# Where the scratch writes of weights stand in a fused attention and gated-MLP kernel

## The chip, the cores and the metric

The kernel runs on one core of a Trainium2 chip. Its time is the device time of one execution in microseconds (us), a median over runs. The core has TensorE (matrix products; in the profile PE, with its weight loads as PEld), VectorE (DVE), ScalarE (ACT), GpSimd (POOL, almost unused here) and SyncE (SP), whose queue issues nearly all DMAs. SBUF is the memory on the core, PSUM holds the sums that TensorE writes, and DRAM scratch tiles are memory outside the core that the kernel writes and reads again.

## The reference

Chunked attention with a left and right context and eight memory keys, and then RMS normalisation and a gated MLP over its output. All is in 32 bit floats.

```python
for c in range(nc):                       # 24 chunks of 32 queries, for 4 batches x 8 heads
    ...
    scores = scale * np.matmul(q_c, k_full.transpose(0, 1, 3, 2))     # 8 memory keys + up to 56
    scores = scores - np.max(scores, axis=-1, keepdims=True)
    a = np.exp(scores)
    a = a / (np.sum(a, axis=-1, keepdims=True) + 1e-09)
    out[:, :, c_start:c_end] = np.matmul(a, v_full)
...
x = out.transpose(0, 2, 1, 3).reshape(3072, 512)
rms = np.sqrt(np.mean(x * x, axis=-1, keepdims=True) + 1e-06)
xn = x / rms * rms_g
g = xn @ w_gate                           # 512 x 1536
silu = g * (1.0 / (1.0 + np.exp(-g)))
val = xn @ w_val                          # 512 x 1536
return (silu * val @ w_out).astype(np.float32)        # 1536 x 512
```

## The kernel before

**Tiling.** The 3072 tokens are eight blocks of 384. The 1536 hidden features are twelve groups of 128, `f` = 0 to 11. Each fp32 factor is split in a high and a low part, and a product is three passes (high-high, high-low, low-high). For a block, each `f` needs a gate product (tile `pg`, L469), a value product (`pv`, L469), an activation (tanh L483, then VectorE's L487, L490 and the split into `hh` and `hl`, L178 and L499), and an output product (`po`, L519).

**Four parts in order of time.** (1) Blocks 0 and 1, with their attention, by a list of steps written out by hand (`ORDER`); also the weights are split here. (2) The loop over `segments`: the rest of block 0 (f 5 to 11, seven features), all of block 2 (the third block), all of block 3. (3) Blocks 4 and 5 together (`whole(2)`), with a Strassen-like scheme of sums, and then (4) blocks 6 and 7 (`whole(3)`). Parts 3 and 4 read their weights back from DRAM scratch tiles `kept` through a ring of 30 buffers `r`. The scratch tiles are filled during part 2.

**What fills the scratch tiles.** There are twelve items, one for each pair of features `p` (0 to 5) and each of the gate and value weights (`g`, `v`). An item has a plain part and a split part:

- `dumps(k)` writes the plain part: six DMAs straight from the split weights in SBUF (four of `kg` or `kv`, 256 and 128 KB, and two of `ko`, 256 KB; 1280 KB in all; L767). They wait for nothing but their place in SyncE's queue: each call is tied behind the last SyncE instruction written so far. Their order is items 2 to 11, then 0 and 1 (the pair of features 10 and 11).
- `keep_steps` makes the split part, in eight steps an item: two additions (VectorE, L803), four quarter steps (VectorE, L806; after the fourth ScalarE copies into `kh`, L810), and two subtractions (L815), the last of them with two DMAs of 512 KB (L817 from `kh`, L819 from `ks` or `qp`). `kh` is a single buffer. The sums alternate between two buffers (`ks` and a part of `qp`). The last two steps of an item come after the first two of the next. A step has a size (512, or 256 for a quarter step), and `keep(n)` draws steps until `n` is used up.

**Gaps and visits.** In part 2, `visit(2 * n)` comes after the gate product of the n-th feature of the block, `visit(2 * n + 1)` after its value product, and `visit(2 * n + 1.5)` after the output product of the feature before. These places are called gaps. At a gap stand, in this order, `dumps`, `keep` and steps of the attention of later blocks, by `VISITS`: "p" (transposes `pT`, L279), "s" (the scores of a pair of units, L216, then loads of queries and keys of the next pair into the same buffers, L163 and L165), "o" (the outputs `oe` and `oo`, L310, and loads of values, L170) and "n" (steps of the normalisation). The query and key buffers (`q`, `qp`, `kv`) exist once for each unit of a pair, so a load waits until the scores of the pair before have been read.

**What sets the order.** TensorE's instructions keep the program's order. For VectorE, ScalarE and SyncE a planner orders them at build time by a simulated timeline, within the dependencies, the priorities and the ties that the program gives (`tc.issue_after`). On the chip each engine runs its own list in order.

`KEEP[blk][gap]` holds the sizes for `keep`. The plain parts have no table; `visit` says

```python
if blk == 0 and gap in range(12):
    dumps((gap + 2) % 12)
keep(KEEP[blk].get(gap, 0))
```

Of the kernel before, what the change touches and what calls it, by code (L numbers as in the profile page):

```python
# [8 lines left out]
F32 = mybir.dt.float32  # L9
# [14 lines left out]
DM, FF = 512, 1536  # L24
P = 128
# [22 lines left out]
NR = 30  # L48

KEEP = {0: {2: 1024, 3: 1024},  # L50
# [3 lines left out]

CHAIN = (("g", 1, "a", 1), ("g", 2, "c", 1), ("v", 1, "a", 1), ("g", 6, "a", 0), ("v", 2, "c", 1), ("g", 7, "a", 0),
         ("v", 6, "a", 0), ("g", 5, "e", 1), ("g", 4, "a", 0), ("v", 7, "a", 0), ("g", 3, "e", 0), ("v", 5, "e", 1),
# [30 lines left out]
def tile_kernel(ctx: ExitStack, tc: tile.TileContext, q, k, v, w_gate, w_val, w_out, rms_g, out):  # L87
# [11 lines left out]
    dram = ctx.enter_context(tc.tile_pool(name="dram", bufs=1, space=bass.MemoryType.DRAM))  # L99
# [174 lines left out]
    def stage_p(u, tag=None):  # L274
        d = st[u]
        t = psum_m(tag, f"pT{u}") if tag else psum_a(f"pT{u}")
        pe = d["p"].rearrange("p j k -> p (j k)")
        for i in range(NT):
            on_pe(nc.tensor.transpose(out=t[:, i * P:(i + 1) * P], in_=pe[:, i * P:(i + 1) * P], identity=ident))  # L279
        d["t"] = t  # L280
# [183 lines left out]
    def moe_in(n, f, xs, kts=range(NKT), ps=None):  # L464
        if ps is None:
            ps = psum_m(n, f"p{n}")
        for kt in kts:
            for i, (a, c) in enumerate(PASS):
                on_pe(nc.tensor.matmul(ps[:, 0:HT], lhsT=weight(a, n, f, kt), rhs=xs[c][:, kt],  # L469
                                 start=kt == 0 and i == 0, stop=kt == NKT - 1 and i == 2))  # L470
        return ps[:, 0:HT]
# [37 lines left out]
    def moe_h(g, vv, blk):  # L509
        t = moe_t(g, vv, blk)  # L510
        return moe_hl(t, moe_hh(t))

    def psm_o(i):
        return psum_m(f"o{i}", f"po{i}")

    def moe_out(f, h, po, first=0, end=NF - 1):
        for i in range(NT):
            for n, (a, c) in enumerate(PASS):
                on_pe(nc.tensor.matmul(po[i], lhsT=h[a][:, i * P:(i + 1) * P], rhs=weight(c, "o", f),  # L519
                                 start=f == first and n == 0, stop=f == end and n == 2))  # L520
# [4 lines left out]
    def store(blk, po):  # L525
        for i in range(NT):
            o = obuf(f"ob{i}")
            nc.scalar.activation(o, po[i], AF.Copy, scale=0.5 if blk > 1 else sh[blk][:, i:i + 1])
            nc.scalar.dma_start(out=out[blk * HT + i * P:blk * HT + (i + 1) * P], in_=o)
# [23 lines left out]
    def last_of(eng):  # L553
        return next(i for i in reversed(nc.cur_bb.bb.instructions) if i.engine == eng.engine)
# [136 lines left out]
    def tok_o(n):  # L691
# [10 lines left out]
        P=lambda n: stage_p(n, "o0" if n < NG else None),  # L702
# [58 lines left out]
    kept = {}  # L761

    def dump(f, w, cols, to):
        k, i, n = fgroup[f]
        for part in range(2):
            c = wt[part, w, k].bitcast(F32)[:, i * DM:(i + 1) * DM]
            nc.sync.dma_start(out=to[:, :, part], in_=c[:, cols].rearrange("p (k f) -> p k f", k=to.shape[1]))  # L767

    items, sums = [(p, w) for p in (5, 0, 1, 2, 3, 4) for w in "gv"], {}

    def dumps(k):
        p, w = items[k]
        fa, fb = PAIRS[p]
        kept[w, p] = t = dram.tile([P, 7, 2, DM // 2], F32, name=f"k{w}{p}")
        with tc.issue_after(last_of(nc.sync)):
            dump(fa, w, slice(0, DM), t[:, 0:2])
            dump(fb, w, slice(DM // 2, DM), t[:, 2:3])
            f = fa if w == "g" else fb
            kept["o", f] = t = dram.tile([P, 2, DM], F32, name=f"ko{f}")
            dump(f, "o", slice(0, DM), t.unsqueeze(1))  # L780

    def keep_steps():

        late_part = iter(())
        for k in range(len(items) + 1):
            now = keep_item(k) if k < len(items) else iter(())
            for _ in range(2):
                if k < len(items):
                    yield next(now)
            yield from late_part  # L790
            if k < len(items):
                for _ in range(4):
                    yield next(now)
            late_part = now

    def keep_item(k):
        p, w = items[k]
        fa, fb = PAIRS[p]
        s = (late["tmp"] if k % 2 else p1.tile([P, 2 * DM], F32, name="ks", tag="wy")).rearrange("p (k f) -> p k f", k=4)
        for i, f in enumerate((fb, fa)):  # L800
            c, n, _ = fgroup[f]
            h, l = (wt[part, w, c][:, n * DM:(n + 1) * DM].bitcast(F32).rearrange("p (k f) -> p k f", k=2) for part in range(2))
            nc.vector.tensor_tensor(out=s[:, 2 * i:2 * i + 2], in0=h, in1=l, op=ALU.add)  # L803
            yield DM
        for o, a, b, op in ((1, 0, 1, ALU.add), (0, 2, 0, ALU.subtract), (2, 1, 2, ALU.subtract), (3, 3, 2, ALU.subtract)):
            nc.vector.tensor_tensor(out=s[:, o], in0=s[:, a], in1=s[:, b], op=op)  # L806
            if o == 3:
                h = p1.tile([P, 3 * HT], F32R, name="kh", tag="rg")[:, 0:2 * DM].rearrange("p (k f) -> p k f", k=4)
                for i in range(4):
                    nc.scalar.copy(h[:, i], s[:, i])  # L810
            yield DM // 2
        l, t = s.bitcast(F32R), kept[w, p]
        for i in range(2):
            c = slice(2 * i, 2 * i + 2)
            nc.vector.tensor_tensor(out=l[:, c], in0=s[:, c], in1=h[:, c].bitcast(F32), op=ALU.subtract)  # L815
            if i:
                nc.sync.dma_start(out=t[:, 3:7, 0], in_=h.bitcast(F32))  # L817
                with tc.issue_after(last_of(nc.sync)):
                    nc.sync.dma_start(out=t[:, 3:7, 1], in_=s)  # L819
            yield DM  # L820

    keeping = keep_steps()

    def keep(n):
        with tc.issue_after(last_of(nc.vector)), tc.issue_after(last_of(nc.scalar)):
            while n > 0:
                n -= next(keeping, DM)
# [150 lines left out]
    for blk, fs in segments:  # L978
        po = [psm_o(i) for i in range(NT)] if blk else sp["po", 0]
        edge = dict(first=fs[0] if blk else 0, end=fs[-1])  # L980

        def visit(gap):
            if blk == 0 and gap in range(12):
                dumps((gap + 2) % 12)
            keep(KEEP[blk].get(gap, 0))
            for c in VISITS[blk].get(gap, ""):
                if next(todo) != c:
                    raise AssertionError(gap)
        for n, f in enumerate(fs):
            g = moe_in("g", f, xs)  # L990
            visit(2 * n)
            out_ = lambda f=fs[n - 1], h=prev: moe_out(f, h, po, **edge)
            if n == 0:
                out_ = lambda: None
                if blk == 0:

                    moe_out(NF - 1, prev, po1)
                    with tc.high_priority():
                        store(1, po1)
            vv = moe_in("v", f, xs)  # L1000
            visit(2 * n + 1)
            if n < len(fs) - 1:
                out_()
                visit(2 * n + 1.5)
                prev = moe_h(g, vv, blk)
                if blk == 3 and n == 2:
                    late_cm[1].__exit__(None, None, None)
                if blk == 3 and n == 7:
                    w0_cm.__exit__(None, None, None)
                    xpool = ctx.enter_context(tc.tile_pool(name="xs", bufs=1, reuse_waits="tile"))  # L1010
                    sup["ring"] = ctx.enter_context(tc.tile_pool(name="ring", bufs=NR, reuse_waits="tile"))
                    for m in (1, 2, 3, 6):
                        sup["xpool", m] = xpool
                    load(NR)
                    x_first(4)
                if blk == 3 and n == 9:
                    x_second(4)
            elif blk < 3:
                with tc.high_priority():
                    t = moe_t(g, vv, blk)  # L1020
                xs = split_x(late_x["x"], t, out_, lambda h: moe_out(fs[-1], h, po, **edge))
            else:
                with tc.high_priority():
                    h = moe_h(g, vv, blk)
                out_()
        if blk == 0:
            behind.close()
        if blk < 3:
            store(blk, po)
# [84 lines left out]
```

## Time and profile before

| | |
|---|---|
| median of 3 runs | 696.56 us (696.29 to 696.63) |
| the profiled execution | 696.32 us, of which the span from first to last instruction is 694.5 us |
| granted TensorE clock, mean | 0.993 |
| TensorE busy | 667.8 us (96%) |
| VectorE, ScalarE busy | 471.5 us (68%), 305.0 us (44%) |
| DMA queue of SyncE | 77760 packets, 136.08 MB, 58.6% of 16 engines' span |
| the stage from 147.2 to 212.75 us (rest of block 0) | 65.55 us; TensorE busy 59.76, VectorE 41.43, ScalarE 20.22; DMA engines 98% busy, 335 GB/s |

The page gives busy times by engine, then 40 equal slices of the span, each with its busy share in tenths (here 17.4 us a slice), then DMA queues, the chain of work that ended last, and the costliest groups of instructions. Lists of waits say who waited for whom: total us, how often, and the longest. A timeline's row has start, duration, engine (SPq is SyncE's DMA queue, where the duration is that of issuing), line of the kernel, operation and tiles (written <- read), count, and in brackets the idle time before it with what ended it. A table of stretches has the length, then busy time of TensorE, its weight loads, VectorE, ScalarE and GpSimd with counts, then the granted TensorE clock, the DMA share and GB/s.

### The profile page before, as it was taken

What the parts mean: (1) busy time and instruction counts of PE and PEld (TensorE: products, weight loads), DVE (VectorE), ACT (ScalarE), POOL (GpSimd) and SP (SyncE); (2) the same over time, 40 slices, a digit from 0 to 9 for tenths busy, and PEclk for the clock granted to TensorE, in tenths of its full rate; (3) what the DMA queues carried; (4) which work ended last, traced back from release to release, by engine and by line L of the source; (5) the groups of instructions that cost most, each with busy time, mean ns of one, the idle gap of its engine ahead of it and who ended that gap; (6) DMA issues with size and microseconds to landing.
All of it is one profiled execution on the core that took longest, in us unless ns stands there. A gap on an engine that the chain in (4) does not pass through costs nothing.

```text
span 694.5 us, 15083 instructions
## 1 busy us (share of the span) xinstructions
PE 667.8 (96%) x6134; PEld 609.5 (88%) x6134; DVE 471.5 (68%) x937; ACT 305.0 (44%) x566; POOL 4.7 (1%) x12
## 2 busy tenths in 40 slices
PE   7799999999699999999999999999999999999997
PEld 6698899998598898889999899998988899999885
DVE  6788999867478898867858766569639254555221
ACT  4787987832235444344234444343334343332112
POOL 0010000000000000000000000000000000000000
PEclk9999999999999999999999999999999999999999
DMA  9653643449996746337139688887643598885002
GB/s 326 248 179 126 238 156 106 148 153 371 322 375 233 232 152 203 116 99 254 58 108 356 234 255 282 266 294 237 192 143 123 177 301 252 251 254 160 0 1 91
DMA packets 79701, 140.19 MB, mean 202 GB/s; under 512 B 7440, under 2 KB 33040, under 8 KB 79632
## 3 DMA queue, kind: packets, MB, share of 16 engines
q1 hardware_dynamic: 77760, 136.08, 58.6%
q10 hardware_dynamic: 1872, 3.15, 1.2%
q8 instruction: 48, 0.79, 0.5%
q14 instruction: 21, 0.17, 0.1%
HBM read 104.60 MB, written 34.60 MB: 200 GB/s over the span
## 4 chain that ended last, share of the span: by engine, by line
PE 75%; DVE 11%; DMA 5%; ACT 5%; issue 2%; SPq 1%; ACTq 0%; DVEq 0%
PE po L957 14%; PE pv L469 10%; PE pg L469 10%; PE po L519 10%; PE mga L928 7%; PE mva L928 7%; PE mve L928 3%; PE mge L928 3%; PE oe L310 2%; PE mvc L928 2%; PE s L216 2%; PE pT L279 2%; DMA r<-kg 1%; PE mgc L928 1%; DVE t L487 1%
## 5 line engine op out<-in xcount | busy, mean ns | idle before, releaser
L957 PE MATMUL po<-r,hhs 128*128 128x512 f32 x288 | 90.7, 396 | 0.0
L469 PE MATMUL pv<-xh,wh_v 128*128 128x384 f32 x192 | 65.8, 343 | 2.2 <-DVE t L490 1.3
L469 PE MATMUL pg<-xh,wh_g 128*128 128x384 f32 x192 | 66.7, 347 | 0.4 <-DVE t L487 0.4
L469 PE MATMUL pg<-xl,wh_g 128*128 128x384 f32 x192 | 65.4, 341 | 0.5 <-DVE xl L654 0.5
L469 PE MATMUL pv<-xh,wl_v 128*128 128x384 f32 x192 | 65.1, 339 | 0.5 <-DVE wl_v L440 0.5
L469 PE MATMUL pg<-xh,wl_g 128*128 128x384 f32 x192 | 65.5, 341 | 0.0
L469 PE MATMUL pv<-xl,wh_v 128*128 128x384 f32 x192 | 65.1, 339 | 0.0
L957 PEld LDWEIGHTS po<-r,hhs 128*128 128x128 f32 x288 | 53.9, 188 | 12.4
L519 PE MATMUL po<-wh_o,hh 128*128 128x512 f32 x144 | 58.3, 405 | 0.8 <-ACT hh L753 0.4
L928 PE MATMUL mga<-x,r 128*128 128x384 f32 x288 | 58.3, 337 | 0.2 <-ACT spare L900 0.2
L928 PE MATMUL mva<-x,r 128*128 128x384 f32 x288 | 58.1, 337 | 0.1
L519 PE MATMUL po<-wh_o,hl 128*128 128x512 f32 x144 | 57.4, 398 | 0.0
L519 PE MATMUL po<-wl_o,hh 128*128 128x512 f32 x144 | 57.2, 397 | 0.0
L957 PE MATMUL po<-r,hls 128*128 128x512 f32 x144 | 56.8, 395 | 0.0
L939 DVE TENSOR_TENSOR hls<-h,hhs 128x768 fp32r<-128x768 f32 x24 | 22.9, 955 | 42.1 <-ACT hhs L938 42.1
L928 PEld LDWEIGHTS mga<-x,r 128*128 128x128 f32 x288 | 50.5, 188 | 1.0 <-ACT spare L900 0.5
L928 PEld LDWEIGHTS mva<-x,r 128*128 128x128 f32 x288 | 50.5, 188 | 0.5 <-DVE h L911 0.4
L178 ACT CAST hh<-t 128x384 fp32r<-128x384 f32 x46 | 23.7, 514 | 47.4 <-PE po L519 35.7
L938 ACT CAST hhs<-h 128x768 fp32r<-128x768 f32 x24 | 20.0, 835 | 54.4 <-PE po L957 50.5
L469 PEld LDWEIGHTS pv<-xh,wh_v 128*128 128x128 f32 x192 | 36.3, 189 | 4.0 <-DVE t L490 1.6
L469 PEld LDWEIGHTS pg<-xh,wh_g 128*128 128x128 f32 x192 | 36.3, 189 | 2.8 <-DVE t L487 0.9
L469 PEld LDWEIGHTS pg<-xl,wh_g 128*128 128x128 f32 x192 | 36.4, 189 | 2.1 <-DVE xl L654 0.7
(162 smaller groups left out, 1424.6 us busy)
## 6 DMA issues: line engine op xcount, KB each, us to landing
r<-kg SPq DMA_DIRECT2D x84, 256.0 KB, 3.3
r<-kv SPq DMA_DIRECT2D x84, 256.0 KB, 3.3
r<-ko SPq DMA_DIRECT2D x48, 256.0 KB, 3.1
kv<-in_v_dram SPq DMA_DIRECT2D x24, 384.0 KB, 5.3
kv<-in_k_dram SPq DMA_DIRECT2D x24, 312.0 KB, 4.7
ws<-in_moe_w_gate_dram SPq DMA_DIRECT2D x4, 1024.0 KB, 4.9
ws<-in_moe_w_val_dram SPq DMA_DIRECT2D x4, 1024.0 KB, 4.9
ws<-in_moe_w_out_dram SPq DMA_DIRECT2D x4, 1024.0 KB, 5.0
```

Of the source, the lines that this page charges most:

```text
L178: return nc.scalar.copy(out, in_)
L216: on_pe(nc.tensor.matmul(d["s"][a:a + CH, o:o + KC], lhsT=d["q"][r, c * CH:c * CH + CH], rhs=d["k"][r, c // 2, 40 * cp:40 * cp + KC], star ...
L279: on_pe(nc.tensor.transpose(out=t[:, i * P:(i + 1) * P], in_=pe[:, i * P:(i + 1) * P], identity=ident))
L310: on_pe(nc.tensor.matmul(o2[cp][64 * hh:64 * hh + 64, o:o + CH], lhsT=st[u]["v"][r, j, hh], rhs=pt[r, j, hh ^ u % 2], start=True, stop=True))
L469: on_pe(nc.tensor.matmul(ps[:, 0:HT], lhsT=weight(a, n, f, kt), rhs=xs[c][:, kt], start=kt == 0 and i == 0, stop=kt == NKT - 1 and i == 2))
L487: nc.vector.scalar_tensor_tensor(out=t, in0=t, scalar=1.0, in1=g, op0=ALU.add, op1=ALU.mult)
L519: on_pe(nc.tensor.matmul(po[i], lhsT=h[a][:, i * P:(i + 1) * P], rhs=weight(c, "o", f), start=f == first and n == 0, stop=f == end and n = ...
L928: on_pe(nc.tensor.matmul(bank[w, b], lhsT=r[:, a, kt], rhs=x[:, c, kt], start=bool(first) and kt == 0 and i == 0, stop=kt == 1 and i == 2, ...
L938: nc.scalar.copy(hh, sup["h", f])
L939: nc.vector.tensor_tensor(out=hl, in0=sup["h", f], in1=hh.bitcast(F32), op=ALU.subtract)
L957: on_pe(nc.tensor.matmul(po[i], lhsT=cur[a][:, i * P:(i + 1) * P], rhs=r[c], start=f == n == 0, stop=f == NF - 1 and n == 2))
```

## The change

The items still go out in the same order, but by a table `DUMPS` of gaps. Before, gaps 0 to 11 of block 0 each had an item. Now gaps 0, 1, 2 and 6 to 12 of block 0 have the first ten, and gaps 1 and 2 of block 2 have the two of features 10 and 11. The scratch tiles are named ahead of the loop. The table `KEEP` has other sizes in blocks 2 and 3, so that some steps of the split parts move by a gap or more; their sequence is the same. Which steps a gap draws, from the generator, where they differ most (the item's pair and weight, then the step):

| gap | before | after |
|---|---|---|
| block 2, gap 0 | 5v first addition | 5v both additions |
| block 2, gap 16 | 3v four quarter steps, 4g additions | 3g last subtraction and write, 3v two quarter steps |
| block 2, gap 18 | 3v first subtraction | nothing |
| block 3, gap 2 | 3v last subtraction and write, 4g two quarter steps | 3v two quarter steps, 4g additions |
| block 3, gap 3 | 4g two quarter steps, 4v additions, 4g first subtraction | 3v subtractions and write, 4g four quarter steps |
| block 3, gap 4 | 4g last subtraction and write, 4v four quarter steps and first subtraction | 4v additions |
| block 3, gap 6 | 4v last subtraction and write | 4g first subtraction |
| block 3, gap 10 | nothing | 4g last subtraction and write, 4v four quarter steps, subtractions and write |

```diff
 KEEP = {0: {2: 1024, 3: 1024},
-        2: {0: 512, 1: 2048, 2: 2048, 3: 2048, 4: 2048, 6: 512, 7: 1024,
-            8: 2048, 9: 2048, 10: 2048, 11: 2048, 12: 2048, 13: 2048, 14: 2048, 15: 2048, 16: 2048, 18: 512},
-        3: {2: 1024, 3: 2048, 4: 2048, 6: 512, 10: 1024}}
+        2: {0: 1024, 1: 2048, 2: 2048, 3: 2048, 4: 1024, 6: 512, 7: 1024, 8: 2048, 9: 2048, 10: 2048, 11: 2048, 12: 2048, 13: 2048,
+            14: 2048, 15: 2048, 16: 1024},
+        3: {2: 1536, 3: 2048, 4: 1024, 6: 512, 10: 3072}}
+
+DUMPS = {0: (0, 1, 2, 6, 7, 8, 9, 10, 11, 12), 2: (1, 2), 3: ()}
...
-    items, sums = [(p, w) for p in (5, 0, 1, 2, 3, 4) for w in "gv"], {}
+    items = [(p, w) for p in (5, 0, 1, 2, 3, 4) for w in "gv"]
+    for p, w in items:
+        kept[w, p] = dram.tile([P, 7, 2, DM // 2], F32, name=f"k{w}{p}")
 
     def dumps(k):
+        k = (k + 2) % len(items)
         p, w = items[k]
         fa, fb = PAIRS[p]
-        kept[w, p] = t = dram.tile([P, 7, 2, DM // 2], F32, name=f"k{w}{p}")
+        t = kept[w, p]
         with tc.issue_after(last_of(nc.sync)):
...
-    keeping = keep_steps()
+    keeping, dumping = keep_steps(), iter(range(len(items)))
...
         def visit(gap):
-            if blk == 0 and gap in range(12):
-                dumps((gap + 2) % 12)
+            if gap in DUMPS[blk]:
+                dumps(next(dumping))
             keep(KEEP[blk].get(gap, 0))
```

## The prediction

> **What bounds the kernel now.** I read the page first, then TensorE's list of waits, then the stretch around its longest wait in the timelines of TensorE and SyncE. The page:
>
> ```profile
> span 694.5 us, 15083 instructions
> PE 667.8 (96%) x6134; PEld 609.5 (88%) x6134; DVE 471.5 (68%) x937; ACT 305.0 (44%) x566; POOL 4.7 (1%) x12
> PE   7799999999699999999999999999999999999997
> DVE  6788999867478898867858766569639254555221
> DMA  9653643449996746337139688887643598885002
> ```
>
> TensorE is busy 96% of the span, so only its idle time is to be won. Between its first and its last slices it falls in one alone, the eleventh (174 to 191 us), to 6; there VectorE falls to 4 and the DMA engines stand at 9. That is the stage in which block 0's last part runs and all the scratch writes are issued. Its waits, over the whole run (total, times, longest):
>
> ```profile
> PE s L216 <- DMA kv<-in_k_dram: 5.3, 2, 3.8
> ...
> PE pv L469 <- ACT xT L321: 0.8, 1, 0.8
> ```
>
> The first row is two waits, 5.3 us in sum, of an attention pair's scores for a key load. TensorE's timeline and the chain that ended last show two visits that do the same work, gap 5 (no wait) and gap 7 (both waits):
>
> ```profile
> 169.95 0.82 PE L279 MATMUL pT<-ident,pe 128*128 128x128 f32 x6
> ...
> 180.24 0.82 PE L279 MATMUL pT<-ident,pe 128*128 128x128 f32 x6
> 184.86 0.30 PE L216 MATMUL s<-kv,q 64*32 64x64 f32 x4 [3.79 <-DMA kv<-in_k_dram]
> 186.68 0.32 PE L216 MATMUL s<-kv,qp 64*32 64x64 f32 x2 [1.52 <-DMA kv<-in_k_dram]
> ...
> 192.79 0.44 PE L469 MATMUL pg<-xh,wh_g 128*128 128x384 f32 x1
> ```
> ```profile
> 170.76 1.10 PE s L216 x72
> 171.87 2.31 PE po L519 x9
> ...
> 175.97 2.31 PE pg L469 x12
> ...
> 180.65 5.89 DMA kv<-in_k_dram
> ...
> 186.68 1.58 PE s L216 x87
> 188.25 2.99 PE po L519 x9
> ```
>
> From the transposes to the next gate matmul, gap 5 takes 175.97 - 169.95 = 6.02 us and gap 7 192.79 - 180.24 = 12.55 us. The difference, **6.53 us**, is what the waits cost: 3.79 + 1.52 = 5.31 us of waiting and 1.22 us of slower work behind it. SyncE's queue says why the load was late:
>
> ```profile
> 162.94 0.38 SPq L767 DMA_DIRECT2D kg<-wh_g  x1
> ...
> 166.71 0.50 SPq L767 DMA_DIRECT2D kv<-wh_v  x1
> ...
> 179.19 0.40 SPq L163 DMA_DIRECT2D q<-in_q_dram  x1
> ...
> 181.18 0.85 SPq L170 DMA_DIRECT2D kv<-in_v_dram  x2
> 182.08 0.73 SPq L767 DMA_DIRECT2D kg<-wh_g  x1
> ...
> 191.78 0.41 SPq L163 DMA_DIRECT2D q<-in_q_dram  x1
> ...
> 194.78 1.04 SPq L767 DMA_DIRECT2D kg<-wh_g  x1
> ...
> 212.31 0.37 SPq L817 DMA_DIRECT2D kg<-kh  x1
> ```
>
> The pair's buffers come free at 171.87, when gap 5's scores end. The loads leave only from 179.19 on, since SyncE works in order and until then issues the items of gaps 3, 4 and 5 (from 166.71). The last key load leaves at 180.65 and takes 5.89 us; the scores could have begun at 184.86 - 3.79 = 181.07.
>
> **The change part by part.** Times go against the profiled execution: 694.5 us of span, 696.32 us in all. The median of the runs, 696.56, is 0.24 above it.
>
> *Removed* from in front of the loads: the items of gaps 3, 4 and 5, 18 DMAs. Gap 2's item is out by 166.7; SyncE then waits for the scores, and the last key load leaves 180.65 - 179.19 = 1.5 us after the first, at 173.4. How long loads and writes of this buffer took in this stage, at least, in the middle and at most:
>
> ```profile
> DMA to landing us min/median/max: 2.9/4.6/6.8
> ```
>
> At the worst the last key lands at 180.2, before 181.07: both waits go. The value loads behind wait for the end of gap 5's output matmuls (175.97), are issued by 176.9 and land by 183.7 at the worst; gap 7's output needs them 1.10 + 2.31 us after 181.1, at 184.5. So nothing is late next in this visit. The slower work goes with the wait, as the granted clock (third from the end) says:
>
> ```profile
> 186.70:188.30 1.60, 1.60 (x93) 1.43 (x93) 0.04 (x1) 0.00 (x0) 0.00 (x0) 0.50 1.06 383
> 188.30:191.20 2.90, 2.90 (x13) 2.06 (x13) 1.91 (x4) 0.68 (x2) 0.00 (x0) 0.75 1.08 389
> ```
>
> After the idle time the clock is 0.50, then 0.75; the scores took 1.58 for 1.10 us and the output 2.99 for 2.31. The Trainium skill (TensorE: Matmul & The Clock Gate, Part 1: The HAM clock gate) says that one idle window of about 3.4 us halves the clock and that about 3.4 us of sustained work restores it. By its figure the slow stretch would cost 3.4 x 0.5 = 1.7 us, an estimate, and the visit 7.0 us in place of 6.53; the rows are shorter, and they decide. Term: **-6.53**. VectorE lets TensorE keep it: at 4 tenths in this slice it has no backlog, and the norm chain behind gap 7 begins with TensorE's outputs, so it moves along.
>
> *Moved:* five items (six DMAs each) now follow gap 7's loads, in gaps 8 to 12, and one each stands in block 2's gaps 1 and 2. Only the last stage reads them. But the first write of split parts (kh, the row at 212.31) is queued behind gap 1's item, the second behind gap 2's too, and kh has one buffer: ScalarE's next copies into it wait until the write has landed. ScalarE, VectorE, TensorE and the landing times of kh's writes:
>
> ```profile
> 220.48 0.71 ACT L810 CAST kh<-qp 128x256 fp32r<-128x256 f32 x2
> 221.58 0.49 ACT L483 ACTIVATE t<-pg 128x384 f32<-128x384 f32 x1 [0.39 <-PE pg L469]
> ```
> ```profile
> 223.56 0.55 DVE L487 SCALAR_TENSOR_TENSOR t<-t,pg 128x384 f32<-128x384 f32 x1
> ...
> 277.88 1.29 DVE L803 TENSOR_TENSOR ks<-wh_g,wl_g 128x512 f32<-128x512 f32 x2 [1.38 <-DMA kg<-ks]
> ```
> ```profile
> 215.23 2.10 PE pg L469 x12
> ...
> 225.74 2.12 PE pg L469 x12
> ```
> ```profile
> DMA to landing us min/median/max: 2.9/3.0/6.2
> ```
>
> Four items took SyncE 212.31 - 194.78 = 17.5 us, 4.4 each; a set of loads took 194.78 - 191.78 = 3.0. From 176.9 on: two items 8.8, loads 3.0, six items 26.3, so kh's write leaves at 215.0. With a short queue an item needs less (166.71 - 162.94 = 3.8), so I put it at 213 to 215, landing 3.0 later, at 216 to 218. With the compute 6.53 earlier the copies are due at 220.48 - 6.53 = 213.95. If ScalarE keeps its order, they are held 2 to 4 us, and the tanh behind them (221.58) too. VectorE's step on the gate bank (223.56) ends at 224.1 and TensorE takes that bank again at 225.74: 1.6 us are covered, 0.4 to 2.4 pass through. If the planner puts the copies later, nothing does. No row decides between 0 and 2.4; I take **+0.8**, below the middle, since the planner orders ScalarE with the DMAs in view. The second item could hold 0g's copies by its own 3.8 us; I take that as covered, and price it in rival A.
>
> *Shifted:* the sequence of the keep steps stays, only their gaps change. Block 2's gap 16 gives the last two quarter steps of 3v and the two additions of 4g to block 3, gap 18 a subtraction. The additions are the row at 277.88: 1.38 us of waiting for a scratch write and 1.21 of work, ahead of the softmax of a pair, behind which ScalarE copies xT; TensorE waits 0.8 us for that copy (second row of the waits). With 2.6 us out of the way this wait goes: **-0.8**; at the worst nothing is won. In block 3, gaps 2 to 6 hold fewer steps in sum and gap 10 takes seven: the end of 4g and six of 4v. Their prices, and two stretches from that gap on (TensorE, its loads, VectorE, ScalarE after the length):
>
> ```profile
> L806 DVE TENSOR_TENSOR ks<-ks x24: 409/417/426, 162.7 to 311.3; 128x256 f32<-128x256 f32 x24
> ...
> L815 DVE TENSOR_TENSOR ks<-ks,kh x12: 681/683/692, 215.8 to 318.7; 128x512 fp32r<-128x512 f32 x12
> ```
> ```profile
> 343.00:354.00 11.00, 10.80 (x236) 9.51 (x235) 8.43 (x23) 4.73 (x10) 0.00 (x0) 1.00 0.45 142
> 354.00:367.00 13.00, 13.00 (x237) 11.63 (x237) 5.76 (x11) 3.37 (x8) 0.00 (x0) 1.00 0.24 75
> ```
>
> Four quarter steps and three subtractions are 4 x 0.42 + 3 x 0.68 = 3.7 us of VectorE, which has 11.00 - 8.43 = 2.6 free there and 7.2 behind. That free time hides them, and 3.7 would be the price without it. I take **+0.2**.
>
> Sum: -6.53 + 0.8 - 0.8 + 0.2 = -6.3. 696.32 - 6.3 = 690.0; with the 0.24 to the median, **690.2 us**.
>
> **The rivals.**
>
> *A: the backlog of writes comes back in block 2.* For it: the DMA engines stand at 9 through this whole stage, and the split writes come due 6.5 us earlier than before while the queue does not empty earlier. Against it: the cover of 1.6 us, and that ScalarE's order is planned anew. If kh holds TensorE for 2.4 us and the second item for 3.8 - 1.6 = 2.2 more, the cost is 4.6 in place of 0.8: 694.0.
>
> *B: the change doesn't do what it says.* Gap 6's and gap 7's items wait for nothing, the loads for TensorE. If those two items were issued ahead of the loads, these would leave at 166.7 + 8.8 = 175.5, the last at 177.0, landing 5.89 later at 182.9: 1.8 us of waiting stay, and the time is 692.0. Only with 4.5 us of new waits from ScalarE's and VectorE's new order on top would it be no change. Against it: in the rows above the loads stand behind the items of the gaps ahead of them and ahead of those that follow.
>
> *C, slower: block 2's two items stand wholly in ScalarE's path.* If 5v's and 0g's copies each wait for a whole item without cover, two items at (191.78 - 182.08) / 2 = 4.85 cost 9.7 us: 696.56 - 6.53 + 9.7 = 699.7. It decides from 6.5 + 1.4 = 7.9 us of such waits. Against it: the cover, and that kh's write landed in 3.0 us in the middle.
>
> **How the numbers follow.** About 0.2%, 1.4 us, is what a measurement of this kernel can tell from no change. My forecast has its own range from 688.4 (kh hidden, gap 10 hidden, and some 1 us of other waits gone) to 691.5 (kh at 2.4 us): chance 0.71. A and the usual form of B, 691.5 to 695: 0.20. B with as much lost elsewhere, no change: 0.05. C: 0.04. So faster 0.91, same 0.05, slower 0.04. The range takes in most of A: 688.0 to 693.6.
>
> **What would show it.** Right: no wait of L216 for a key load; the four loads leave just behind gap 5's scores, near 172, with no L767 between gap 2's item and them; no clock below 1.00 near 185; block 2's first gate matmuls, now at 215.23, near 208.7. The price of kh: ScalarE's copies into kh waiting for kh's write near 214, and TensorE idle between 212 and 225. Block 2's end: TensorE's wait for xT gone. Gap 10: L806 and L815 between 335 and 355 with TensorE at work. Wrong: a wait of L216 that stays, or one of about its length that stands behind it.

## The result and the profile after

The changed kernel takes 700.61 us (median of 5 runs, 700.12 to 701.27), the kernel before 696.63 (696.29 to 698.4) beside it: a ratio of 1.0053, 95% interval 1.0038 to 1.0068. It is **slower by 0.5%** where 0.9% faster was forecast. The profiled execution took 700.12 us, its span is 698.3. First the page: the span, and two rows of slices (17.5 us each):

```profile
span 698.3 us, 15072 instructions
PE 668.6 (96%) x6134; PEld 611.9 (88%) x6134; DVE 470.5 (67%) x937; ACT 304.8 (44%) x566; POOL 4.7 (1%) x12
PE   7899999999997999969999999999999999999997
DMA  9654644358999556152258788888644598875002
```

The dip of TensorE has left the eleventh slice, as predicted. Two new dips stand later: the thirteenth slice (209 to 227 us) at 7 and the eighteenth (297 to 314 us) at 6. The list of TensorE's waits names them (total, times, longest):

```profile
PE pv L471 <- ACT xT L323: 7.2, 2, 5.7
PE pg L471 <- DVE t L489: 4.5, 1, 4.5
```

The first row is two waits: 5.65 us in the eighteenth slice and the nineteenth, and 1.60 us behind block 2's gap 5, which is taken up below. L471, L323, L489 and L281 are the lines that were L469, L321, L487 and L279 before. No row names a key load any more. **Gap 7** (TensorE, then SyncE's queue):

```profile
168.70 0.81 PE L281 MATMUL pT<-ident,pe 128*128 128x128 f32 x6
178.72 0.82 PE L281 MATMUL pT<-ident,pe 128*128 128x128 f32 x6
```
```profile
165.28 0.45 SPq L769 DMA_DIRECT2D ko<-wl_o  x1
170.61 0.33 SPq L165 DMA_DIRECT2D q<-in_q_dram  x1
...
172.15 0.43 SPq L167 DMA_DIRECT2D kv<-in_k_dram  x1
174.39 1.77 SPq L172 DMA_DIRECT2D kv<-in_v_dram  x2
176.22 0.43 SPq L769 DMA_DIRECT2D kv<-wh_v  x1
```

The loads leave at 170.61 to 172.15, with no item between gap 2's last write and them: 8.6 us earlier than before (1.25 of that because the kernel came to gap 5 earlier), and gap 7's scores wait for nothing. This part of the prediction held.

**Block 0's store**, first new stall. The timeline of all engines, in order of time, and the chain that ended last at the same place:

```profile
205.85 0.69 ACT L530 ACTIVATE ob<-po,srh 128x512 f32<-128x512 f32 x1
...
212.21 0.37 ACTq L531 DMA_DIRECT2D out_dram<-ob  x1
212.68 1.26 ACT L530 ACTIVATE ob<-po,srh 128x512 f32<-128x512 f32 x2 [6.14 <-DMA ko<-wl_o]
...
214.75 0.49 ACT L485 ACTIVATE t<-pg 128x384 f32<-128x384 f32 x1 [0.81 <-ACT ob L530]
215.28 0.55 DVE L489 SCALAR_TENSOR_TENSOR t<-t,pg 128x384 f32<-128x384 f32 x1 [5.41 <-ACT t L485]
215.88 0.69 PE L471 MATMUL pg<-xh,wh_g 128*128 128x384 f32 x1 [4.48 <-DVE t L489]
...
218.15 1.32 ACT L815 CAST kh<-qp 128x256 fp32r<-128x256 f32 x4 [2.90 <-DMA kg<-kh]
```
```profile
208.62 3.51 DMA ko<-wl_o
...
212.15 0.02 ACTq L531
...
215.88 3.68 PE pg L471 x12
```

ScalarE has the first third of block 0's output ready at 205.85 + 0.69 = 206.54. The DMA that stores it (L531) is issued by ScalarE itself, and leaves only at 212.21. The chain shows what releases it: a write of the plain part of weights, `ko<-wl_o`, that SyncE issued at 208.62 and that landed 3.51 us later, at 212.13. It has no data in common with the store. ScalarE waits 5.67 us for it (206.54 to 212.21), and is idle for 6.14 with the issue of the store behind. ScalarE works in order, so behind the store wait its next copy, the tanh (214.75), VectorE's gate step (215.28) and TensorE (4.48 us). Behind the wait the gate product takes 3.68 us where 2.10 is usual: 1.58 more, 6.06 in all.

**Block 3's gap 3**, second new stall; timeline of all engines, and chain:

```profile
307.07 0.42 SPq L167 DMA_DIRECT2D kv<-in_k_dram  x1
307.59 0.39 SPq L822 DMA_DIRECT2D kv<-kh  x1
...
311.06 0.46 ACT L323 COPY xT<-oe 128x384 f32<-128x384 f32 x1
314.12 1.32 ACT L815 CAST kh<-ks 128x256 fp32r<-128x256 f32 x4 [2.60 <-DMA kv<-kh]
315.35 0.47 ACT L323 COPY xT<-oo 128x384 f32<-128x384 f32 x1
...
315.87 0.69 PE L471 MATMUL pv<-xh,wh_v 128*128 128x384 f32 x1 [5.65 <-ACT xT L323]
```
```profile
307.59 6.45 DMA kv<-kh
...
315.87 4.21 PE pv L471 x12
```

The write of item 3v from `kh` leaves behind the loads of gap 1 and lands at 314.04. The new table has put 4g's quarter steps right behind it, and the planner has put their four copies into `kh` (L815) between the two copies of `xT`. `kh` has one buffer, so the first of them waits for that write, and the second `xT` copy, for which TensorE stands, waits behind all four. TensorE's 5.65 us of waiting are followed by a value product of 4.21 us where 2.11 is usual: 2.10 more, 7.75 in all.

**Behind block 2's gap 5** stands a third and smaller wait (TensorE):

```profile
237.69 0.44 PE L471 MATMUL pv<-xh,wh_v 128*128 128x384 f32 x1 [1.60 <-ACT xT L323]
```

The kernel before waits for `xT` only once, at block 2's end (0.8 us). Whose wait this is, e9 shows below.

To place the whole difference, TensorE's rows of `pT` (as the two shown for gap 7) give the stretches between the same visits, in us:

| kernel | gap 5 to 7 | gap 7 to block 2, gap 5 | block 2, gap 5 to 17 | to block 3, gap 1 | to block 3, gap 5 | to part 3 |
|---|---|---|---|---|---|---|
| before | 10.29 | 49.59 | 42.72 | 33.23 | 15.86 | 75.35 |
| after | 10.02 | 49.10 | 43.74 | 31.36 | 23.88 | 74.91 |
| after - before | -0.27 | -0.49 | +1.02 | -1.87 | +8.02 | -0.44 |

They sum to +5.97; the time up to gap 5 (-1.25) and from part 3 on (-0.92) make it the +3.8 of the spans. The time up to gap 5 differs between executions of the same program: the changed kernel came to gap 5 at 168.70 us in its profile, and e5 below, the same program up to block 3, at 172.13. So the stretches say more than one span. The second column hides two large numbers: gap 7 gave its 6.53 and the store took 6.04. The third holds the wait of 1.60.

### The profile page after: what moved, and what is told of

It reads as the page before. It is cut to its first block, busy times and chain, and to the rows that moved or that the text cites. A ratio compares the mean times of both kernels' runs of the same rounds, so it can differ in the third digit from the quotient of the medians.

```text
span 698.3 us, 15072 instructions
## 1 busy us (share of the span) xinstructions
PE 668.6 (96%) x6134; PEld 611.9 (88%) x6134; DVE 470.5 (67%) x937; ACT 304.8 (44%) x566; POOL 4.7 (1%) x12
## 3 DMA queue, kind: packets, MB, share of 16 engines
q10 hardware_dynamic: 1872, 3.15, 1.2%
## 4 chain that ended last, share of the span: by engine, by line
PE 81%; DVE 6%; ACT 5%; DMA 4%; SPq 2%; issue 2%; POOL 0%; ACTq 0%; DVEq 0%
PE po L962 14%; PE pv L471 12%; PE pg L471 11%; PE po L521 11%; PE mga L933 7%; PE mva L933 7%; PE mve L933 4%; PE mge L933 4%; PE mvc L933 2%; PE s L218 2%; PE oe L312 2%; PE mgc L933 2%; PE pT L281 2%; SPq L769 1%; DMA kv<-in_v_dram 1%
## 5 line engine op out<-in xcount | busy, mean ns | idle before, releaser
L471 PE MATMUL pv<-xh,wh_v 128*128 128x384 f32 x192 | 66.3, 345 | 9.2 <-ACT xT L323 7.2
L471 PE MATMUL pg<-xh,wh_g 128*128 128x384 f32 x192 | 67.7, 352 | 4.5 <-DVE t L489 4.5
L471 PE MATMUL pv<-xh,wl_v 128*128 128x384 f32 x192 | 65.7, 342 | 0.5 <-DVE wl_v L442 0.5
L471 PE MATMUL pg<-xl,wh_g 128*128 128x384 f32 x192 | 65.7, 342 | 0.0
L471 PE MATMUL pv<-xl,wh_v 128*128 128x384 f32 x192 | 65.6, 342 | 0.0
L471 PE MATMUL pg<-xh,wl_g 128*128 128x384 f32 x192 | 65.6, 342 | 0.0
L471 PEld LDWEIGHTS pv<-xh,wh_v 128*128 128x128 f32 x192 | 36.6, 190 | 10.9 <-ACT xT L323 7.9
L471 PEld LDWEIGHTS pg<-xh,wh_g 128*128 128x128 f32 x192 | 36.8, 192 | 7.5 <-DVE t L489 5.3
L471 PEld LDWEIGHTS pg<-xl,wh_g 128*128 128x128 f32 x192 | 36.8, 192 | 1.3
```

## The experiments

Two stories: *theory S*, the two stalls above cost the time, and each can be taken away alone; and rivals that are named with each run. All ratios are to runs of the kernel before on the same chip in the same job. The expectations use S, K, D and A as short names; what each says is in the text. The stretches of all runs:

| kernel | ratio, 95% interval | gap 7 to block 2, gap 5 | block 2, gap 5 to 17 | to block 3, gap 1 | to block 3, gap 5 |
|---|---|---|---|---|---|
| items only (e1) | 0.9982 (0.9963 to 1.0001) | 45.54 | 42.91 | 34.23 | 17.36 |
| keep table only (e2) | 1.0003 (0.9984 to 1.0022) | 49.35 | 42.39 | 31.37 | 19.01 |
| after, store by SyncE (e3) | 1.0054 (1.0029 to 1.0079) | 43.68 | 47.08 | 31.36 | 23.83 |
| e1, store by SyncE (e4) | 0.9982 (0.9954 to 1.0010) | 44.25 | 46.41 | 34.56 | 17.35 |
| after, 4g one gap later (e5) | 0.9944 (0.9922 to 0.9965) | 49.06 | 43.75 | 31.36 | 16.90 |
| five items late, old table (e7) | 0.9903 (0.9873 to 0.9933) | 43.65 | 42.05 | 33.17 | 17.39 |
| five items late, new table (e8) | 0.9888 (0.9859 to 0.9917) | 43.70 | 42.42 | 31.37 | 19.11 |
| five items late, new table, 4g later (e6) | 0.9873 (0.9850 to 0.9896) | 43.44 | 42.41 | 31.36 | 17.56 |
| after, two items late (e9) | 0.9895 (0.9857 to 0.9932) | 45.50 | 42.42 | 31.38 | 17.93 |
| e9 and 4g later (e10) | 0.9901 (0.9868 to 0.9934) | 45.24 | 42.43 | 31.38 | 17.69 |

**The two halves of the change apart (e1, e2).** e1 is the changed kernel with the old `KEEP`; e2 is the kernel before with the new `KEEP` and no `DUMPS`.

> The changed kernel with the old table KEEP, so only the scratch items of plain parts move. Theory S (two new stalls: ScalarE's output DMA behind block 0 waits for the landing of gap 12's item, worth 6.1 us of TensorE with the slower clock behind it; and, from KEEP alone, ScalarE's copies into kh in block 3 wait for kh's write, worth 7.4): the first stall stays, the second goes, so 696.6 - 6.9 + 6.1 = 695.8 us, with a wait of 4 to 5 us of TensorE for L489 near 215 and none of some 5 us for xT near 316. Rival K (KEEP's new order is the whole loss): 696.6 - 6.9 = 689.7 us. Rival D (the moved items are the whole loss, by whatever way): 700.6 us.

> The kernel before with the new table KEEP alone; the scratch items stay where they were. Theory S: the wait of gap 7 stays and no wait arises at ScalarE's output DMA; kh's wait of block 3 comes, at most 7.4 us, and some 1 us is won at the end of block 2: 695.5 to 702.7 us. In this kernel's instruction list both copies of xT stand ahead of the copies into kh, so what waits is what stands behind them (squares and the tanh), and the cost may be well below 7.4. Rival K: 696.6 + 11 = 707 us or so. Rival D: 696 us.

Measured: 696.36 us for e1 and 698.01 for e2, beside 697.22. Each half alone is about no change; together they lose 0.5%. So rival K (689.7 and about 707 us) and rival D (700.6 and 696) are out. e1's time is near the 695.8 us of theory S, but not by its parts: its stall at the store is 2.20 us where 4 to 5 were expected, and block 2's end and block 3's stretch are 1.0 and 1.5 us longer than before. e1 keeps gap 7's gain. Its stall at the store, from TensorE's timeline:

```profile
215.81 0.44 PE L471 MATMUL pg<-xh,wh_g 128*128 128x384 f32 x1 [2.20 <-DVE t L489]
```

e2 wins 1.9 us at the end of block 2 and loses 3.15 in block 3, where its planner set 4g's copies behind both `xT` copies: there they hold the squares and the tanh, not `xT` (ScalarE and TensorE):

```profile
315.63 0.41 ACT L810 CAST kh<-ks 128x256 fp32r<-128x256 f32 x1 [3.00 <-DMA kv<-kh]
...
318.81 0.45 PE L469 MATMUL pg<-xh,wh_g 128*128 128x384 f32 x1 [1.61 <-DVE t L487]
```

So the wait for `kh`'s write comes with the table, and its price (3.15 or 8.0 us) with the order that the planner finds around it. The two halves don't add up: the planner sees both.

**The store taken off ScalarE's queue (e3, e4).** In e3 (the changed kernel) and e4 (e1) SyncE issues block 0's store:

```diff
-            nc.scalar.dma_start(out=out[blk * HT + i * P:blk * HT + (i + 1) * P], in_=o)
+            (nc.scalar if blk else nc.sync).dma_start(out=out[blk * HT + i * P:blk * HT + (i + 1) * P], in_=o)
```

> The changed kernel with block 0's output DMAs issued by SyncE in place of ScalarE. Theory S: ScalarE no longer waits for the landing of an item, the wait of TensorE for L489 near 215 goes, and the time is 700.6 - 6.1 = 694.5 us; the wait near 316 stays. Rival A (kh's write is queued behind the items, and ScalarE's copies into kh hold TensorE anyway): ScalarE waits for kh near 214 and TensorE loses 2 to 4 us there, 696.5 to 698.5 us.

> The changed kernel with the old table KEEP and block 0's output DMAs issued by SyncE. Theory S: both new stalls are gone and the won wait of gap 7 stays: 689.7 us, up to 692 if kh near 214 costs something. Rival (the time won in gap 7 is lost anyway later, since the writes need their time): 695 us or more.

Measured: 700.58 and 697.54. The planner also sets the store ahead of block 2's first item in SyncE's queue. The stall at the store is gone (49.10 to 43.68 and 45.54 to 44.25), and the time does not move: the next stretch is longer by 3.3 and 3.5 us. That leaves 2.1 us won in e3 and 2.2 lost in e4, which the times, with intervals of about 0.25% to either side, don't tell from nothing. e3's timeline of all engines:

```profile
222.62 0.40 SPq L822 DMA_DIRECT2D kv<-kh  x1
...
226.38 1.33 ACT L815 CAST kh<-ks 128x256 fp32r<-128x256 f32 x4 [2.11 <-DMA kv<-kh]
...
236.76 0.69 PE L471 MATMUL pv<-xh,wh_v 128*128 128x384 f32 x1 [3.68 <-ACT xT L323]
```

The write of 5v from `kh` leaves at 222.62, behind block 2's two items; the copies into `kh` wait for it, VectorE's steps follow late, and TensorE waits behind block 2's gap 5 for `xT`, 3.68 us where the changed kernel waits 1.60 (2.69 in e4). My numbers for both runs were too good by the whole gain: I had taken the store for the one thing that was late. e3's rival (696.5 to 698.5) was too good as well, e4's (695 or more) was right. That is rival A of the prediction in kind: the same bytes stand in the same queue until about 222 us, and whoever needs it next pays.

**One step group later in block 3 (e5).** The sizes of `KEEP[3]` at gaps 3 and 6 move 4g's four quarter steps from gap 3 to gap 4, and 4v's additions from gap 4 to gap 6:

```diff
-        3: {2: 1536, 3: 2048, 4: 1024, 6: 512, 10: 3072}}
+        3: {2: 1536, 3: 1024, 4: 1024, 6: 1536, 10: 3072}}
```

> The changed kernel, with one thing moved in block 3: the four quarter steps of item 4g stand one gap later (gap 3 keeps only 3v's two subtractions and its write; gap 4 still has 1024, now 4g's quarter steps; 4v's additions go to gap 6). Theory S (the wait at block 3's fourth gap comes from ScalarE's copies into kh, which wait there for 3v's write to land between the two copies of xT): the wait of TensorE for xT (5.65 us in the changed kernel) goes or falls under 1 us, the stretch from block 3's gap 1 to gap 5 takes 16 to 17.5 us in place of 23.9, and the time is 6 to 7 us below that of the changed kernel, 693 to 695 us beside 697 for the kernel before in the same job. Rival (the wait comes from VectorE having more steps of 4g and 3v in this stage, whatever kh does): the steps only change gaps by one, so the stretch stays above 21 us and the time above 698.

Measured: 694.2 us beside 698.31. The stretch falls from 23.88 to 16.90, and the copies of `xT` stand together again (ScalarE, then TensorE):

```profile
313.80 0.46 ACT L323 COPY xT<-oe 128x384 f32<-128x384 f32 x1
314.16 0.48 ACT L323 COPY xT<-oo 128x384 f32<-128x384 f32 x1
...
320.45 0.87 ACT L815 CAST kh<-ks 128x256 fp32r<-128x256 f32 x2 [0.96 <-DVE ks L811]
```
```profile
314.70 0.44 PE L471 MATMUL pv<-xh,wh_v 128*128 128x384 f32 x1 [1.05 <-ACT xT L323]
```

The wait is 1.05 us, just above the 1 us that was expected at most, and the stretch 1.04 above the kernel before. With the same quarter steps one gap later 6.98 of the 8.02 us are gone: the second stall was the place of the copies against `kh`'s write, not VectorE's load. 4v's additions, which leave the stretch, are too small to explain that (1.29 us for the two additions in the prediction's row at 277.88), and in e9 below no step is moved and most of the stall is gone too. The rival is out.

**Fewer bytes before block 2 (e7, e8, e6).** The last five items stand at the end of block 2, where the DMA engines have room (1 tenth in the changed kernel's seventeenth slice, 279 to 297 us): with the old `KEEP` (e7), the new one (e8), and the new one with e5's edit (e6).

```diff
-DUMPS = {0: (0, 1, 2, 6, 7, 8, 9, 10, 11, 12), 2: (1, 2), 3: ()}
+DUMPS = {0: (0, 1, 2, 6, 7, 8, 9), 2: (17.5, 18, 19, 19.5, 20), 3: ()}
```

> The table of the keep steps is that of the kernel before; the plain items are where the changed kernel has them up to gap 9 of block 0, and the other five stand at gaps 17.5, 18, 19, 19.5 and 20 of block 2, where the DMA engines were at 1 to 2 tenths of their time, instead of gaps 10 to 12 of block 0 and 1 and 2 of block 2. Theory S (what was won at gap 7 is lost since the same bytes are squeezed in between there and block 2's gap 5, where either block 0's store or kh's write is late): gap 7's wait stays away, block 0's store and kh's first writes are not late, the stretch from gap 7's transposes to block 2's gap 5 is 43 to 44 us (49.6 before, 49.1 in the changed kernel), and the time is 690 to 691.5 beside 697. Rival D (the queue is as full anyway, or the late items delay block 2's store, block 3's loads or 3v's write by as much): 694 to 698, with a wait of TensorE of 3 us or more after block 2's gap 17.

> The same late items as in the run before, with the changed kernel's table of keep steps. Theory S: block 2's end gives its 1.9 us (stretch from gap 17 to block 3's gap 1 at 31.4 us in place of 33.2), while ScalarE's copies of 4g into kh still stand between the two copies of xT at block 3's gap 3 and wait for 3v's write; how long depends on what is queued ahead of that write (3.2 us more without items near, 8.0 in the changed kernel). So 691 to 694, that is 1 to 3 us above the run with the old table. Rival K (the table alone costs nothing; the 8 us came from the items' place): the stretch from gap 1 to gap 5 of block 3 is under 17 us and the time is 688 to 690.

> Late items as in the two runs before, the changed kernel's table, and 4g's quarter steps one gap later. Theory S: gap 7's 6.5 us and block 2's end's 1.9 us are kept and nothing of block 3 is lost: 688 to 689.5 beside 697, the best of the four. Rival D (late items hold a write or a load in block 3): a new wait of TensorE of 2 us or more between block 2's gap 17 and block 3's gap 11, and 691 to 695.

Measured: 692.5, 690.7 and 689.58 us beside 698.31. In all three the stretch behind gap 7 is 43.4 to 43.7 (before, without its stall, 49.59 - 6.53 = 43.06), the store leaves right behind its copy, and the longest wait for `kh` up to block 2's gap 5 is 0.47 us (e7). So rival D is out. The late items also shift the rotation of counters that is explained below; what the counter alone does at the store, e9 shows. e8 still pays for 4g's copies in block 3 (19.11), so rival K is out too; e6 does not. But e8 came out 1.8 us under e7, not 1 to 3 above it, and its copies stand behind both `xT` copies, not between them. e7's and e6's times are 1.0 and 0.08 us above what was expected, beside a kernel before that was 1.3 above. e6 has the lowest median of all versions, 1.3% under the kernel before (0.985 to 0.9896); its interval overlaps with those of e7 to e10. Its wait for `xT` (it was 7.2), and the store, which leaves 0.03 us behind the copy:

```profile
PE pv L471 <- ACT xT L323: 0.5, 1, 0.5
```
```profile
208.51 0.69 ACT L530 ACTIVATE ob<-po,srh 128x512 f32<-128x512 f32 x1
209.23 0.34 ACTq L531 DMA_DIRECT2D out_dram<-ob  x1
```

**Why the store waited for a foreign write (e9, e10).** The instruction list of the changed kernel, as built, shows that a DMA's completion is counted in one of eight counters (DMAHW0 to DMAHW7), given out in rotation over the DMAs of SyncE's and ScalarE's queues together, and that a DMA waits until the one before it on its counter has landed. From that list, the last write of gap 11's and of gap 12's items and block 0's store:

```
L769 DMA ko_2459<-wl_o_1087 128x512 [waits DMAHW7_49]
...
L769 DMA ko_2501<-wl_o_1093 128x512 [waits DMAHW5_49]
...
L531 DMA out_dram<-ob_2554 128x512 [waits DMAHW5_49,Activation_49]
```

The store shares counter 5 with gap 12's last write, eight DMAs ahead in the planned order. Six of the DMAs between are block 2's first item. If these go, the store falls on counter 7, gap 11's last write, though the queue ahead of it is the same. e9 does that (`2: (18, 19)` in place of `2: (1, 2)` in `DUMPS`); e10 adds e5's edit.

> The changed kernel, but with block 2's two plain items at gaps 18 and 19 in place of 1 and 2. Everything that stands ahead of block 0's store in SyncE's queue stays. In the instruction list as built the store's first DMA now shares its completion counter with gap 11's last write (the one that leaves at 205.12 in the changed kernel) and not with gap 12's last write (208.62), as there are eight counters in rotation and six DMAs fewer ahead of it in the planned order. Theory S with the counter: the store leaves some 3.5 us earlier against ScalarE's copy ahead of it, ScalarE's wait falls from 6.1 to 2 or 3 us, TensorE's wait for VectorE's gate step from 4.5 to 0.5 to 1.5, and the stretch from gap 7's transposes to block 2's gap 5 from 49.1 to 43.5 to 45.5 us; the wait at block 3's gap 3 stays (stretch 19 to 24). Time 3 to 6 us under that of the changed kernel, 693 to 697.5 beside 697 to 698 for the kernel before. Rival Q (the store waits because the queue ahead of it is full, not because of the counter): writes that are issued behind the store can't free it, so ScalarE's wait stays at 5 to 6 us and TensorE's at 3.5 or more.

> As the run before, and with item 4g's four quarter steps one gap later in block 3. Theory S: both stalls are mended by moving two items and four steps of the changed kernel; the stretch from block 3's gap 1 to gap 5 is 16 to 17.6 us, and what is left of the wait at the store 0.5 to 1.5: 688.5 to 692 beside 697 to 698. Rival Q: the store's 4 to 6 us stay and the time is 693 to 695.

Measured: 691.38 and 690.88 us beside 697.56; 693 to 697.5 and 688.5 to 692 were expected. e9, all engines in order of time:

```profile
208.75 0.69 ACT L530 ACTIVATE ob<-po,srh 128x512 f32<-128x512 f32 x1
209.70 0.34 ACTq L531 DMA_DIRECT2D out_dram<-ob  x1
210.02 0.45 SPq L769 DMA_DIRECT2D ko<-wl_o  x1
```

The store leaves at 209.70, before gap 12's last write (210.02) has even been issued. A store that waited for the queue ahead of it to empty could not go that early; one that waits for the counter can, so rival Q is out. e9 also shows whose the third wait was: with block 2's two items away TensorE waits 0.42 us there, and that stretch falls from 43.74 to 42.42. In e10, whose block 0 ran 1.5 to 1.9 us earlier, the store waits again a little, for the write that the new counter names (chain, then ScalarE):

```profile
205.32 3.26 DMA ko<-wl_o
```
```profile
209.10 1.27 ACT L530 ACTIVATE ob<-po,srh 128x512 f32<-128x512 f32 x2 [1.56 <-DMA ko<-wl_o]
...
214.68 1.33 ACT L815 CAST kh<-qp 128x256 fp32r<-128x256 f32 x4 [3.02 <-DMA kg<-kh]
```

The second row is the wait for `kh` that the prediction had in mind: of it TensorE loses 0.97 and 0.79 us, at the next gate product and at block 2's first transposes, and the stretch is 2.2 us above 43.06. In e9 ScalarE waits 3.71 us for `kh`, and the stretch is 2.4 above.

```profile
219.94 0.44 PE L471 MATMUL pg<-xh,wh_g 128*128 128x384 f32 x1 [0.97 <-DVE t L489]
225.22 0.87 PE L281 MATMUL pT<-ident,pe 128*128 128x128 f32 x6 [0.79 <-DVE t L489]
```

One miss in e9's favour: I expected 19 to 24 us in block 3, where nothing was edited; it took 17.93. The planner had set the copies behind both `xT` copies there, as in e2 and e8. So the 8 us of block 3 need both: 4g's steps at that gap, and a planned order that puts them between the two copies, as in the changed kernel and e3. Which detail of the plan tips that order was not tried, nor a second `kh` buffer. With two items late (e9, e10) and with five (e6 to e8) the times are the same within their intervals.

## Why the prediction was wrong

It said 690.2 us, faster; measured were 700.61, slower. By its terms:

- **Gap 7, -6.53: right.** The waits and the slow stretch behind them went; from the transposes to the next gate product gap 7 fell from 12.55 us to 6.02 (178.72 to 184.74).
- **The moved items, +0.8, bounds 0 to 2.4: this step failed.** I asked who waits for writes that are queued behind the moved items, and named one, `kh`. I did not look at who else issues DMAs in that stage. ScalarE issues block 0's store, and it stands in the same rotation of counters. ScalarE waited 5.67 us there, and the stretch lost 6.04. `kh` itself was sized too low: ScalarE waited 2.90 us for it just behind (row at 218.15), without loss for TensorE there only as the store's stall had given its write time. Without that stall it cost 2.2 to 2.4 us, the upper bound of the term, with block 2's two items away (e9, e10), and 3.3 to 3.5 with them in place (e3, e4). The two items also cost 1.3 us behind block 2's gap 5 (43.74 in the changed kernel, 42.42 in e9). The term had taken the second item as covered; which copies carry its delay to TensorE was not followed.
- **Block 2's end, -0.8: right in kind**, worth 1.87: no wait for `xT` is left there, and TensorE is busy for the whole stretch.
- **Block 3, "gaps 2 to 6 hold fewer steps in sum", no price: this step failed too.** I counted steps and not their place. 3v's write and 4g's copies into the same single buffer came to stand in one gap, and that cost 8.02 us with the planned order of the changed kernel, and 2.07 to 3.25 with the order of e2, e8 and e9. The front of this document shows both in the row of gap 3.
- **Gap 10, +0.2: right.** TensorE's wait there is 0.51 us (0.2 before), and VectorE has hardly anything free any more: busy 10.66 of 11.00 us in the stretch that was 343 to 354 before and comes 5.15 us later here (TensorE, loads, VectorE after the length).

```profile
348.15:359.15 11.00, 10.49 (x235) 9.20 (x234) 10.66 (x28) 6.11 (x14) 0.00 (x0) 1.00 0.65 205
```

Of the rivals, C gave 699.7, near the time by luck: its 9.7 us were all to be lost in block 2, and 8.02 were lost in block 3. It named the right engine and the right items: with block 2's two items away ScalarE was free at the store (e9). But its mechanism, copies into `kh` that wait for a whole item each, is not what the rows show. A, the backlog in block 2, is what e3 and e4 found behind the store. What I got wrong is the chance of anything on that side: 6.5 us were won at a place where the queue had been late, while the bytes ahead of block 2 became fewer by two items of twelve only, and these two stood just behind it.

## What to carry to other kernels

When writes are moved in a full queue, list every DMA of the following stage on every engine's queue, with what each must wait for, before any of them is costed at nothing; the bytes must go to a stage where the queue has room (here the end of block 2: 1.3% for five items, and about 1% for the two that stood next to the store), not to the next gap. When a step moves to another gap, look for the single buffer that it shares with its new neighbours. A gain at one stall is worth its length only if the next consumer of the same resource has slack, and an edit that a planner orders anew should be read from its whole new order, not from the edit.

## What was unexpected on the hardware

A DMA that the compiled program orders only by a shared completion counter held ScalarE for 5.67 us, since the wait stands on the engine that issues the DMA. The Trainium skill (DMA: Bandwidth & Descriptors, Anatomy of one DMA — SWDGE (gpsimd) path) says, for DMAs that GpSimd issues, that a DMA engine doesn't wait on semaphores and that the issuing sequencer does; this trace agrees for one that ScalarE issues: the store's issue waits from 206.54 to 212.21 us, with ScalarE idle.

Idle time has a price behind it. After 4.48 us the changed kernel's clock was 0.61 over the next 3.7 us; after 2.20 us (e1, row above) the gate product ran at 1.00; after 2.69 us e4's clock fell to 0.64 (third from the end in the rows of stretches, of the changed kernel, of e1 and of e4; the row of e4's wait ahead of its own):

```profile
215.88:219.60 3.72, 3.71 (x14) 3.72 (x15) 1.18 (x3) 1.45 (x5) 0.00 (x0) 0.61 1.04 362
```
```profile
215.88:219.60 3.72, 3.72 (x21) 3.72 (x22) 1.85 (x4) 0.72 (x2) 0.00 (x0) 1.00 1.03 355
```
```profile
235.76 0.45 PE L471 MATMUL pv<-xh,wh_v 128*128 128x384 f32 x1 [2.69 <-ACT xT L323]
```
```profile
235.70:238.00 2.30, 2.24 (x8) 2.24 (x9) 2.30 (x9) 1.32 (x4) 0.00 (x0) 0.64 0.93 261
```

The Trainium skill (TensorE: Matmul & The Clock Gate, Part 1: The HAM clock gate) gives one idle window of about 3.4 us; e4's 2.69 us lie below that and were enough, so here the measurement decides.
